# Left tiles at 0 and right tiles at 256 modulo 512 bytes: a wider edge and the constant tile first

## The chip, the cores and the metric

The kernel runs on one core of one Trainium2 chip. The metric is the device time of one execution in microseconds: 654.52 us as the median of three runs before the change (654.43 to 654.73). Engines are named as the profile names them: PE (TensorE matmuls), PEld (its weight loads), DVE (VectorE), ACT (ScalarE), POOL (GpSimd), SP (SyncE, which issues the transfers).

## What is computed

Three layers, one after the other. The first is a chunked linear recurrence over 4 x 8 sequences of 768 tokens ("attention" below), the second an MLP with an ELU, the third a gated MLP.

```python
# attention, per chunk, 8 heads of 32, state 16
CB = einsum('bhin,bhjn->bhij', Cc, Bc)
y  = einsum('bhij,bhjd->bhid', CB * L, xc) + einsum('bhin,bhnd->bhid', Cc, state) * exp(cum)
state = exp(sum(la)) * state + sum_j(Bc xc exp(cum_last - cum_j))
...
x = y as 3072 tokens x 256
h = x @ moe_w_in                          # 256 -> 2048
x = where(h > 0, h, exp(min(h, 0)) - 1) @ moe_w_out      # 2048 -> 256
g = x @ moe2_w_gate ; v = x @ moe2_w_val  # 256 -> 1536 each
out = (g / (1 + exp(-g)) * v) @ moe2_w_out               # 1536 -> 256
```

## The kernel before

The 3072 tokens are six blocks of 512. Work is laid out in a sequence of steps, one for each pair of block b and slice f of 128 features: in **phase 1** (first MLP) 6 x 16 steps, in **phase 2** (gated MLP) 6 x 12. A step issues the matmuls of its own pair and those of the pair LAG = 3 steps back; the attention work for the next block of tokens is put between the steps of phase 1 at fixed offsets, four visits to a block, and so are the decoding and splitting of weights. Engine order is the order in which the code is written (a manual schedule), with semaphores from the tile framework.

Every large product is three fp32r matmuls instead of one fp32 matmul. Each operand is split into a high and a low half (names ending in h and l), and high x high, high x low and low x high are summed. `mm3` (L493) writes these for h, g, v and o, `m_c` (L541) for c. All of them stream 512 columns (the moving operand) against 128 x 128 weights (the stationary operand, loaded anew for each matmul by a PEld instruction). Per step there are:

- phase 1, h (6 matmuls): weights `W1["i", f]` in the tiles w1h and w1l, moving xh and xl;
- phase 1, c (6): weights `W1["o", f]` in the same tiles, moving gh and gl. In block 0 it is instead two fp32 matmuls with `W1["v", f]` (L535);
- phase 2, g (6) and v (6): weights in w2h and w2l, moving x2h and x2l;
- phase 2, o (6): weights in w2h and w2l, moving gh and gl.

Where a tile lies in a partition of SBUF is set by the order in which pools are opened. Pools without a side grow from the left, in this order: `const` (ident8, con, zero_q), x2, `work` (gh, gl, m), w2e, then attention's own; when attention is done, `w2l` (w2h and w2l of f = 0 to 3) and `xs` (x2h and x2l of even blocks) take its place. Pools with `side="right"` grow downwards from the end: `edge`, a tile that nothing reads or writes, then w1p (w1h, w1l), xp (xh, xl), `stage` (raw, e, v). After phase 1 the right is closed as far as the edge, and `w2h` opens there (w2h and w2l of f = 4 to 11, x2h and x2l of odd blocks, yo). So

- h has both operands on the right, c moves from the left and has weights on the right;
- g and v have weights on the left for f < 4 and on the right from there; the moving operand is on the left for even b and on the right for odd b;
- o moves from the left always.

All these tiles are multiples of 512 bytes in size and sliced at multiples of 512, so that a side has one place modulo 512 throughout. The constants: `con` (352 words wide, of which 322 are used) holds two identities, a mask and signs; `ident8` is written once from it (L671) and read by attention's sixteen late scans (L316).

Of the kernel before, what the change touches and what calls it, by code (L numbers as in the profile page):

```python
# [8 lines left out]
F32 = mybir.dt.float32  # L9
# [38 lines left out]
WARM = 0  # L48
LEAD = 4
CON = 352  # L50
EDGE = 24
VB = 2
OX = 13
NW = 3
# [15 lines left out]
def ssm_mlp_glu_kernel(ctx, tc, a, bcs, xbc, w1, w2, consts, out):  # L70
# [4 lines left out]
    const = ctx.enter_context(tc.tile_pool(name="const", bufs=1))  # L75
    x2p = ctx.enter_context(tc.tile_pool(name="x2p", bufs=1))
    work = ctx.enter_context(tc.tile_pool(name="work", bufs=3))

    ident8 = const.tile([128, H, Q], F32, name="ident8")
    con = const.tile([128, CON], F32, name="con")  # L80
    ident_r, ident, blk_sb, sgn_sb = (con[:, x:y] for x, y in ((0, R), (R, R + Q), (R + Q, R + 2 * Q), (R + 2 * Q, R + 2 * Q + 2)))
    zero_q = const.tile([128, Q], F32, name="zero_q")
    x2_all = x2p.tile([128, 2 * NT], F32, name="x2")
# [1 line left out]

    ctx.enter_context(tc.tile_pool(name="edge", bufs=1, side="right")).tile([128, EDGE], F32, name="edge")
    right = ExitStack()
# [744 lines left out]
```

## Time and profile before

| | us |
|---|---|
| median of three runs | 654.52 |
| the profiled execution, whole | 654.61 |
| its span, first to last instruction | 652.8 |
| PE busy | 625.6 (96%) |
| PEld busy | 490.4 (75%) |
| DVE busy | 388.1 (59%) |
| POOL busy | 315.2 (48%) |
| ACT busy | 312.2 (48%) |

The granted clock of TensorE is 1.000 over the span. Matmuls are pipelined: the profile gives one of 512 columns some 390 ns, while the next starts less than 240 ns later. How fast PE goes is therefore read from start to start in the timeline, not from its busy share. In the timeline a row marked x2 stands for two instructions in a row, with the start of the first. For a mean over n gaps the rows give the first and the last start.

### The profile page before, as it was taken

The numbers are of one execution on the slowest core, as the hardware profiler recorded it, in microseconds if no ns is written. First come the engines' busy times: TensorE is split into PE (matmuls) and PEld (weight loads), VectorE is DVE, ScalarE is ACT, GpSimd is POOL, SyncE is SP. The second block draws the span as 40 slices with busy tenths as digits, with TensorE's granted clock in tenths as the row PEclk, the third lists the DMA queues.
The fourth block names the chain that finished last, engine by engine and source line by source line (L and its number), as shares of the span: only waits on it lengthen the run. The fifth ranks groups of instructions, "written<-read, shape, count | busy, mean of one in ns | idle before, by whom it ended". The sixth has DMA issues, their size and how long they took to land.

```text
span 652.8 us, 9659 instructions
## 1 busy us (share of the span) xinstructions
PE 625.6 (96%) x3620; PEld 490.4 (75%) x3620; DVE 388.1 (59%) x580; ACT 312.2 (48%) x562; POOL 315.2 (48%) x263
## 2 busy tenths in 40 slices
PE   2599999999999999999999999999999999999997
PEld 1356667777787778777788888888888888888886
DVE  5869987878887788783574663343343343343332
ACT  2146666666667666666775542322332232332322
POOL 2636657767777577764454332333233333333332
PEclk9999999999999999999999999999999999999999
DMA  6785634454344543410310000000000000000000
GB/s 181 200 286 192 171 111 143 126 151 144 127 133 132 149 133 122 133 33 19 95 50 0 2 1 1 33 0 1 32 1 1 33 1 0 34 0 2 32 1 32
DMA packets 21646, 49.54 MB, mean 76 GB/s; under 512 B 4320, under 2 KB 6496, under 8 KB 21600
## 3 DMA queue, kind: packets, MB, share of 16 engines
q1 hardware_dynamic: 21600, 48.93, 24.1%
q8 instruction: 28, 0.46, 0.3%
q14 instruction: 18, 0.15, 0.1%
HBM read 45.68 MB, written 3.24 MB: 75 GB/s over the span
## 4 chain that ended last, share of the span: by engine, by line
PE 87%; DVE 5%; issue 2%; DMA 2%; ACT 2%; SPq 1%; POOL 0%; POOLq 0%; DVEq 0%; ACTq 0%
PE h L493 18%; PE o L493 15%; PE g L493 15%; PE v L493 15%; PE c L541 14%; PE c L535 4%; DVE E L316 1%; DMA raw<-in_w 1%; PE cb L370 1%; PE y L446 1%; PE y L442 1%; DVE m L521 1%; DVE w2e L140 1%; DMA w2e<-in_xbc 1%; ACT m L515 1%
## 5 line engine op out<-in xcount | busy, mean ns | idle before, releaser
L499 POOL TENSOR_TENSOR gl<-m,gh 128x512 fp32r<-128x512 f32 x152 | 200.1, 1319 | 259.3 <-ACT gh L498 255.5
L613 DVE TENSOR_TENSOR m<-m,g 128x512 f32<-128x512 f32 x72 | 49.5, 688 | 168.5 <-ACT m L608 168.5
L608 ACT ACTIVATE m<-g 128x512 f32<-128x512 f32 x72 | 43.1, 598 | 190.5 <-PE g L493 190.5
L521 DVE SCALAR_TENSOR_TENSOR m<-m,h 128x512 f32<-128x512 f32 x96 | 65.6, 683 | 62.1 <-ACT m L520 62.1
L498 ACT ACTIVATE gh<-m 128x512 fp32r<-128x512 f32 x152 | 94.8, 624 | 1.6 <-DVE m L614 1.0
L515 ACT ACTIVATE m<-h 128x512 f32<-128x512 f32 x96 | 57.1, 595 | 69.1 <-PE h L493 64.5
L493 PE MATMUL h<-xh,w1h 128*128 128x512 f32 x192 | 80.6, 420 | 1.5 <-DVE xl L478 1.0
L493 PE MATMUL h<-xh,w1l 128*128 128x512 f32 x192 | 75.9, 395 | 0.0
L541 PE MATMUL c<-gh,w1h 128*128 128x512 f32 x160 | 63.8, 399 | 1.0 <-DVE x L547 1.0
L541 PE MATMUL c<-gh,w1l 128*128 128x512 f32 x160 | 62.4, 390 | 0.0
L520 ACT ACTIVATE m<-m 128x512 f32<-128x512 f32 x96 | 59.9, 623 | 0.5
L493 PE MATMUL h<-xl,w1h 128*128 128x512 f32 x192 | 59.9, 393 | 0.0
L493 PE MATMUL o<-gl,w2h 128*128 128x512 f32 x144 | 56.7, 394 | 0.0
L493 PE MATMUL g<-x2h,w2h 128*128 128x512 f32 x144 | 56.7, 394 | 0.0
L493 PE MATMUL o<-gh,w2h 128*128 128x512 f32 x144 | 56.6, 393 | 0.0
L493 PE MATMUL o<-gh,w2l 128*128 128x512 f32 x144 | 56.5, 393 | 0.0
L493 PE MATMUL v<-x2h,w2h 128*128 128x512 f32 x144 | 56.5, 392 | 0.0
L493 PE MATMUL g<-x2h,w2l 128*128 128x512 f32 x144 | 56.5, 392 | 0.0
L493 PE MATMUL v<-x2h,w2l 128*128 128x512 f32 x144 | 56.4, 392 | 0.0
L614 DVE TENSOR_TENSOR m<-m,v 128x512 f32<-128x512 f32 x72 | 49.5, 688 | 7.9 <-DVE m L613 0.5
L541 PE MATMUL c<-gl,w1h 128*128 128x512 f32 x160 | 50.4, 396 | 0.0
L493 PEld LDWEIGHTS h<-xh,w1h 128*128 128x128 f32 x192 | 36.4, 190 | 14.4 <-DVE m L521 3.5
(126 smaller groups left out, 1091.3 us busy)
## 6 DMA issues: line engine op xcount, KB each, us to landing
abc<-ac SPq DMA_DIRECT2D x16, 512.0 KB
bcraw<-in_bcs SPq DMA_DIRECT2D x32, 256.0 KB
raw<-in_w SPq DMA_DIRECT2D x15, 512.0 KB
w2e<-in_w SPq DMA_DIRECT2D x12, 512.0 KB
xb<-in_xbc SPq DMA_DIRECT2D x17, 256.0 KB
raw<-in_w SPq DMA_DIRECT2D x12, 256.0 KB
out_y<-yo SPq DMA_DIRECT2D x12, 256.0 KB
abc<-ac SPq DMA_DIRECT2D x8, 128.0 KB
```

Source lines behind the costliest of these rows:

```text
L140: nc.vector.tensor_scalar(halves(v)[:, :, 0], t["h16"][:, :, 1], 13, None, ALU.logical_shift_right)
L493: nc.tensor.matmul(dst, lhsT=l, rhs=r, start=first and i == 0, stop=last and i == len(ops) - 1, **kw)
L498: nc.scalar.activation(hi, src, AF.Copy)
L499: lo_eng.tensor_tensor(lo, src, hi.bitcast(F32), ALU.subtract)
L515: nc.scalar.activation(m, h, AF.Relu, scale=-1.0)
L520: nc.scalar.activation(m, m, AF.Exp, scale=-1.0)
L521: nc.vector.scalar_tensor_tensor(m, m, -1.0, h, ALU.add, ALU.max)
L535: nc.tensor.matmul(cps[b][m], lhsT=W1["v", f][:, m * 128:(m + 1) * 128], rhs=g, start=f == 0, stop=f == NF1 - 1)
L541: nc.tensor.matmul(cps[b][m], lhsT=w[:, m * 128:(m + 1) * 128], rhs=r, start=f == 0 and w is wh and r is gh, stop=f == NF1 - 1 and r is gl)
L608: nc.scalar.activation(m, pg, AF.Sigmoid)
L613: nc.vector.tensor_tensor(m, m, pg, ALU.mult)
L614: nc.vector.tensor_tensor(m, m, pv, ALU.mult)
```

## The change

Two edits. The edge grows from 24 words (96 bytes) to 56 (224 bytes), which moves every right tile down by 128 bytes. And con is allocated before ident8 rather than behind it.

```diff
-EDGE = 24
+EDGE = 56
...
+    con = const.tile([128, CON], F32, name="con")
     ident8 = const.tile([128, H, Q], F32, name="ident8")
-    con = const.tile([128, CON], F32, name="con")
```

The places, as the built programs have them (bytes from the start of a partition, and modulo 512):

| tiles | before | modulo 512 | after | modulo 512 |
|---|---|---|---|---|
| con | 20608 | 128 | 16512 | 128 |
| ident8 | 16512 | 128 | 17920 | 0 |
| zero_q, x2, work (gh, gl), w2e, w2l, xs | 22016 and up | 0 | the same | 0 |
| raw, e, v of stage; xh, xl; w1h, w1l; all of w2h | 132992 and up | 384 | 132864 and up | 256 |

Every engine has the same instructions in the same order as before.

## Rows read from the trace of the kernel before

**Rows 1.** The page's chain that ended last, shares by engine.
```profile
PE 87%; DVE 5%; issue 2%; DMA 2%; ACT 2%; SPq 1%; POOL 0%; POOLq 0%; DVEq 0%; ACTq 0%
```

**Rows 2.** Busy us (instructions) of PE, PEld, DVE, ACT, POOL; clock, DMA, by stretch.
```profile
102.00:345.80 243.80, 242.81 (x1434) 192.52 (x1431) 186.28 (x272) 164.79 (x309) 166.52 (x129) 1.00 0.36 111
345.80:648.90 303.10, 303.10 (x1315) 246.88 (x1314) 121.19 (x165) 97.13 (x167) 95.83 (x74) 1.00 0.03 9
```

**Rows 3.** PE's timeline (start, us, line, out<-moving,weights), block 1, f = 4.
```profile
412.76 0.39 PE L493 MATMUL g<-x2h,w2l 128*128 128x512 f32 x1
...
414.80 0.62 PE L493 MATMUL v<-x2l,w2h 128*128 128x512 f32 x2
```

**Rows 4.** PE's timeline, first matmul of block 2, f = 3 and f = 4.
```profile
457.87 0.39 PE L493 MATMUL g<-x2h,w2h 128*128 128x512 f32 x1
...
461.96 0.40 PE L493 MATMUL g<-x2h,w2h 128*128 128x512 f32 x1
```

**Rows 5.** PE's timeline, block 2: first matmul of f = 5, 7, 11, one more.
```profile
466.14 0.39 PE L493 MATMUL g<-x2h,w2h 128*128 128x512 f32 x1
...
474.50 0.40 PE L493 MATMUL g<-x2h,w2h 128*128 128x512 f32 x1
474.75 0.40 PE L493 MATMUL g<-x2h,w2l 128*128 128x512 f32 x1
...
491.24 0.39 PE L493 MATMUL g<-x2h,w2h 128*128 128x512 f32 x1
```

**Rows 6.** PE's timeline, block 1, f = 0 and 1.
```profile
397.19 0.40 PE L493 MATMUL v<-x2h,w2h 128*128 128x512 f32 x1
397.44 0.40 PE L493 MATMUL v<-x2h,w2l 128*128 128x512 f32 x1
...
399.97 0.40 PE L493 MATMUL g<-x2h,w2h 128*128 128x512 f32 x1
400.21 0.39 PE L493 MATMUL g<-x2h,w2l 128*128 128x512 f32 x1
400.43 0.40 PE L493 MATMUL g<-x2h,w2h 128*128 128x512 f32 x1
...
402.76 0.40 PE L493 MATMUL o<-gh,w2h 128*128 128x512 f32 x1
```

**Rows 7.** PE's timeline, first g and last o of phase 2.
```profile
345.84 0.40 PE L493 MATMUL g<-x2h,w2h 128*128 128x512 f32 x1
...
648.65 0.40 PE L493 MATMUL o<-gl,w2h 128*128 128x512 f32 x1
```

**Rows 8.** PE's timeline, phase 1, between two visits of the attention work.
```profile
127.03 0.40 PE L493 MATMUL h<-xh,w1l 128*128 128x512 f32 x1
...
137.41 0.64 PE L541 MATMUL c<-gl,w1h 128*128 128x512 f32 x2
```

**Rows 9.** PE's timeline, block 0: second h of a run, and what follows the run.
```profile
80.07 0.40 PE L493 MATMUL h<-xh,w1l 128*128 128x512 f32 x1
...
81.23 1.88 PE L535 MATMUL c<-m,v 128*128 128x512 f32 x4
```

**Rows 10.** PE's waits for DVE at L547 (us, times, longest); timeline of one.
```profile
PE c L541 <- DVE x L547: 1.0, 3, 0.6
...
149.17 0.70 DVE L304 TENSOR_TENSOR zc<-bcraw,zc 128x512 fp32r<-128x512 f32 x1
...
156.83 0.68 DVE L547 COPY x<-c 128x512 f32<-128x512 f32 x1
...
157.57 0.50 PE L541 MATMUL c<-gh,w1h 128*128 128x512 f32 x1 [0.58 <-DVE x L547]
```

**Rows 11.** Groups by line: busy us, mean ns of one, idle before.
```profile
L316 DVE TENSOR_TENSOR_SCAN E<-abc,ident 128x1024 f32<-128x1024 f32 x16 | 36.2, 2265 | 0.1
...
L579 ACT ACTIVATE w2h<-w2e 128x768 fp32r<-128x768 f32 x8 | 6.7, 837 | 0.0
...
L579 ACT ACTIVATE w2h<-w2v 128x768 fp32r<-128x768 f32 x4 | 3.3, 836 | 0.0
```

## The prediction

> **What bounds the kernel now.** I read the chain of work that ended last first: 87% of it lies on PE [rows 1]. The table by stretch comes second. In phase 1 after block 0 PE is busy for 242.81 of 243.80 us, in phase 2 for all of 303.10 us, and DVE, ACT and POOL are well below that in both [rows 2]. The granted clock is 1.00 in both, the higher of TensorE's two levels (2.4 GHz). So nobody makes PE wait; what counts is how far apart its matmuls start. I call that distance in time a gap. The busy column doesn't show it, because the recorded matmuls overlap (0.39 us each, starts 0.23 us apart). It has to be read from start times in the timeline, over many matmuls, since one start is given to 10 ns.
>
> Those gaps aren't equal, and they follow the places of the two operands. I write an arrangement as moving/stationary, by the places modulo 512 bytes given in the section on the change.
> - 384/384 (block 1, f from 4): 9 gaps from 412.76 to 414.80 are 2.04 us, 226.7 ns each [rows 3].
> - 0/0 (block 2, f = 3): 18 gaps from 457.87 to 461.96 are 4.09 us, 227.2 ns, a change of arrangement among them [rows 4].
> - 0/384 (block 2, f from 5): 108 gaps from 466.14 to 491.24 are 25.10 us, 232.4 ns [rows 5].
> - 384/0 (block 1, f = 1): 12 gaps from 399.97 to 402.76 are 2.79 us, 232.5 ns [rows 6].
>
> The instruction is the same in all four, as are its shape, the clock and what a step asks of the other engines. In odd blocks f below 4 is slow and f from 4 fast; in even blocks it is the other way round. Only the distance in place between what streams and what is loaded fits that: at distance 0 a gap is 226.7 ns, at 128 and at 384 it is 232.4, so 5.7 ns dearer.
>
> **How many are dear.** Of the 2352 fp32r matmuls (L493 and L541), h (576) has both operands on the right. c (480) streams from the left with weights on the right: dear. In phase 2, g and v have 288 at 0/384, 144 at 384/0, and 432 at distance 0; o has 288 at 0/384 and 144 at 0/0. That is 720 dear ones of 1296 in phase 2 and 1200 in all. 1200 x 5.7 ns = 6.8 us is their direct price. A change of arrangement costs a little more, since the first gaps after it are long.
>
> **What the change does, part by part.** No instruction is added, removed or moved; I cost places alone.
>
> *Right tiles from 384 to 256.* Distances 384 and 128 both become 256; distance 0 stays 0. The trace has no fp32r matmul of 512 columns at 256, so its gap is unknown. Two readings fit the rows. If the cost repeats every 256 bytes, 128 and 384 are one point, which explains why they cost the same, and 256 is the same point as 0: 226.7 ns. If it repeats every 512 and falls away evenly on both sides of 0, 128 and 384 are also alike, and 256 is anything. I take the first. Not only the means are alike at 128 and 384: single gaps of 0.25 us stand among ones of 0.23 on both sides (474.50 to 474.75 [rows 5], 397.19 to 397.44 [rows 6]), so the two arrangements seem to do the same thing in time, which an even falling-away wouldn't need. Bounds for a gap at 256: the nearest rows give 226.7 below and 0.25 us above.
>
> Phase 2: from the first g (345.84) to the last o (648.65) [rows 7] there are 1296 matmuls and 18 c of the last block of phase 1, so 1313 gaps in 302.81 us, 230.6 ns each. At 226.7 they are 297.7 us: **-5.1 us**. (Check: 720 dear ones x 5.7 = 4.1 us; the other 1.0 us is the changes of arrangement, which go as well.)
>
> Phase 1, blocks 1 to 5: 45 gaps between two visits of the attention work, 127.03 to 137.41, are 10.38 us, 230.7 ns [rows 8]. Of 960 matmuls I count some 920 such gaps; each falls by 4.0 ns: -3.7 us. Against that: after a break the gap of distance 0 isn't at once 226.7. In block 0, where h runs six at a time between other matmuls, five gaps take 1.16 us, 232 ns each [rows 9]. Phase 1 has some 24 runs; I charge each up to five gaps of 5 ns, 25 ns, so +0.6 us at most, and take +0.4: **-3.3 us**.
>
> Block 0 and all ahead of it: h is at distance 0 already and is broken up as before. I cost it at **0**; five dear gaps of 5 ns in each of 16 runs, 0.4 us, bound it on both sides.
>
> *What is late next.* PE waits for DVE at ends of blocks: three times, 1.0 us in all, for the copy of c (L547). Before the one at 157.57 DVE works without a pause from 149.17 to the end of that copy [rows 10]. What PE gains in these 8 us it waits off again: 8 us x 4.0/230.7 = 0.14 us for each of up to five block ends, so **+0.5 us** with a little for other local queues. If the whole of phase 1 went at DVE's pace instead, its 3.3 us would be lost; DVE's 186.28 busy of 243.80 [rows 2] speaks against it.
>
> *ident8 from 128 to 0, con 4096 bytes lower.* The sixteen scans that read ident8 take 2265 ns each, 36.2 us [rows 11]; DVE has room in those stretches. No row shows a scan of that size with ident8 elsewhere. I take 0, with 16 x 0.1 us of DVE time as a bound to both sides, hidden but for the local queue above. ACT and DVE also write right tiles: ACT's split of the phase 2 weights takes 837 ns where half of the tiles written lie left and half right, and 836 where all lie right [rows 11], so places don't show there.
>
> Sum: 654.61 - 5.1 - 3.3 + 0.5 = **646.7 us** against the profiled execution (span 652.8, the rest 1.8 around it). The median of the three runs is 0.09 below that execution; that is less than I can tell, and I leave 646.6.
>
> The Trainium skill, "SBUF — State Buffer", section "Who interferes with whom", speaks against any effect: it gives PE two read ports, one for the moving operand and one for LDWEIGHTS, calls them independent, and states that PE and ACT never wait on anyone. By that rule the sum would be 654.5. The trace doesn't agree: 226.7 against 232.4 ns for one instruction in two arrangements.
>
> **The rivals.**
> 1. *No gain.* The fast gap belongs to distance 0 alone, and every other distance costs 232.4. Then 1200 dear matmuls stay dear, the changes of arrangement stay, and the time is 654.5. For it: 128 and 384 are equal. Against it: the same equality is the mark of a pattern of 256 bytes. Nor do places having no part in it at all fit, since the order of fast and slow f turns round between odd and even blocks. 0.07.
> 2. *Slower.* The pattern repeats every 512 bytes and 256, farthest from 0, is its worst point. The place is the same 1200 matmuls. It is slower from a gap above 232.5 on; by 0.2% from 233.6. With the longest single gap read, about 0.24 to 0.25 us, as a constant gap: 1200 x (240 - 232.5) = 9.0 us, 663.5 us. For it: 128 and 384 are worse than 0, so farther could be worse still. Against it: they show alike rhythms, and the smooth worst point would lie at the end of a slope nothing shows. 0.07.
> 3. *Faster still.* 256 is a better point than 0. With the shortest single gap read, 0.22 us (400.21 to 400.43 [rows 6]), as a constant gap: 1200 x (226.7 - 220) = 8.0 us more, 638.6 us. No run of gaps in the rows lies below 226.7. 0.03.
>
> **How the numbers follow.** The forecast, 256 acts as 0, has 0.83. Its own range: if everything above 226.7 vanished in both phases without a charge, 5.1 + 3.7 = 8.8 us and block 0's 0.4 give 645.3; if phase 1 gives nothing, 649.5. With the bound for scans I take 645.0 to 649.8; this leaves out the rivals (0.17) and a little more, and I don't reach for them. About 0.2%, 1.3 us, is what a measurement of this kernel can tell from no change. Faster by more: 0.83 + 0.03 = 0.86; within: 0.07; slower: 0.07.
>
> **What would show it.** In the changed profile: every step of 18 matmuls in phase 2 at 4.08 us, whatever f and block (before 4.10 and 4.19 by turns); the stretch of first g to last o at 297.7 us; 45 gaps of phase 1 at 10.2 to 10.25 us; L547 making PE wait a little longer than 1.0 us in all; the start of phase 1 unchanged. Wrong in the first place: a step of odd block and f below 4, or of even block and f from 4, at 4.18 us or more. Wrong in the second: phase 2 shorter and phase 1 not, with PE's waits grown by some 3 us.

## The result

The changed kernel takes 646.82 us (median of four, 646.32 to 647.07) against 654.47 us (654.24 to 654.73) before: 7.65 us less, a ratio of 0.9882 with an interval of 0.9865 to 0.9899. The prediction was 646.6 us, with a range of 645.0 to 649.8. The profiled execution took 647.0 us with a span of 645.2.

Its page first: the span, the busy times, and the chain that ended last. It answers to [rows 1].

```profile
span 645.2 us, 9659 instructions
...
PE 617.6 (96%) x3620; PEld 490.0 (76%) x3620; DVE 387.9 (60%) x580; ACT 312.0 (48%) x562; POOL 315.1 (49%) x263
...
PE 81%; DVE 8%; DMA 3%; POOL 3%; issue 2%; ACT 2%; SPq 1%; DVEq 0%; POOLq 0%; ACTq 0%
```

The other engines are busy for as long as before; only PE's overlapped time has shrunk, by 8.0 us. PE holds 81% of the chain now instead of 87%, DVE 8% instead of 5%, POOL 3% instead of 0%: at some places the other engines come a little late now.

The table by stretch, as in [rows 2], from the same point in phase 1 to the new start of phase 2, and phase 2:

```profile
102.00:343.40 241.40, 239.76 (x1432) 192.40 (x1431) 186.11 (x272) 164.54 (x309) 166.36 (x129) 1.00 0.37 112
343.40:641.50 298.10, 298.06 (x1315) 246.48 (x1314) 121.08 (x165) 97.18 (x168) 95.78 (x74) 1.00 0.03 9
```

In phase 2 PE has next to no idle time (0.04 us) and the clock is as it was, 1.00. In phase 1 it idles for 1.6 us where it idled for 1.0.

Now the starts on PE's timeline. The first pair is first g and last o of phase 2, as in [rows 7]; the second the first g of block 1 and of block 2; the third a run of phase 1 between two attention visits, as in [rows 8]; the fourth the five gaps of block 0, as in [rows 9].

```profile
343.46 0.39 PE L493 MATMUL g<-x2h,w2h 128*128 128x512 f32 x1
...
641.07 0.39 PE L493 MATMUL o<-gl,w2h 128*128 128x512 f32 x1
...
392.42 0.39 PE L493 MATMUL g<-x2h,w2h 128*128 128x512 f32 x1
...
441.38 0.39 PE L493 MATMUL g<-x2h,w2h 128*128 128x512 f32 x1
...
126.85 0.39 PE L493 MATMUL h<-xh,w1l 128*128 128x512 f32 x1
...
137.07 0.61 PE L541 MATMUL c<-gl,w1h 128*128 128x512 f32 x2
...
80.03 0.39 PE L493 MATMUL h<-xh,w1l 128*128 128x512 f32 x1
...
81.19 0.59 PE L535 MATMUL c<-m,v 128*128 128x512 f32 x1
```

Phase 2 takes 297.61 us from first to last instead of 302.81; its 1313 gaps are 226.7 ns each. Block 1, in which slow and fast f stood side by side, takes 48.96 us for 12 x 18 matmuls, 226.7 ns again, with no dear arrangement left. In phase 1 the 45 gaps take 10.22 us (227.1 ns) instead of 10.38. Block 0 is unchanged at 1.16 us.

Where the 7.6 us of span went: phase 2 gave 5.20. From the first h of block 1 to the first g, 252.17 us (93.67 to 345.84) became 249.82 (93.64 to 343.46): 2.35. The rest, head and tail, is within 0.1.

```profile
93.67 0.79 PE L493 MATMUL h<-xh,w1h 128*128 128x512 f32 x1
```

```profile
93.64 0.79 PE L493 MATMUL h<-xh,w1h 128*128 128x512 f32 x1
```

(The first is of the kernel before, the second of the changed one: block 1's first h.)

### The profile page after: what moved, and what is told of

It is laid out like the page before. It is cut to its first block, busy times and chain, and to the rows that moved or that the text cites. A ratio compares the mean times of both kernels' runs of the same rounds, so it can differ in the third digit from the quotient of the medians.

```text
span 645.2 us, 9659 instructions
## 1 busy us (share of the span) xinstructions
PE 617.6 (96%) x3620; PEld 490.0 (76%) x3620; DVE 387.9 (60%) x580; ACT 312.0 (48%) x562; POOL 315.1 (49%) x263
## 4 chain that ended last, share of the span: by engine, by line
PE 81%; DVE 8%; DMA 3%; POOL 3%; issue 2%; ACT 2%; SPq 1%; DVEq 0%; POOLq 0%; ACTq 0%
PE h L493 16%; PE o L493 15%; PE g L493 15%; PE v L493 15%; PE c L541 12%; PE c L535 4%; DMA raw<-in_w 3%; DVE E L316 1%; POOL xb L340 1%; DVE w2e L140 1%; DVE w2e L143 1%; PE cb L370 1%; PE y L446 1%; DVE m L521 1%; DVE P L334 1%
## 5 line engine op out<-in xcount | busy, mean ns | idle before, releaser
L521 DVE SCALAR_TENSOR_TENSOR m<-m,h 128x512 f32<-128x512 f32 x96 | 65.5, 682 | 60.0 <-ACT m L520 59.9
L520 ACT ACTIVATE m<-m 128x512 f32<-128x512 f32 x96 | 59.9, 624 | 0.5
```

The source lines that it names most:

```text
L520: nc.scalar.activation(m, m, AF.Exp, scale=-1.0)
L521: nc.vector.scalar_tensor_tensor(m, m, -1.0, h, ALU.add, ALU.max)
```

## Experiments: the distance, and which edit

Theory A is the prediction's: a gap's price depends on the distance between the streamed and the loaded operand alone, and repeats every 256 bytes. Theory B: it repeats every 512, and 256 happens to be a good point. Theory C: other users of the moved tiles (ident8's scans, ACT, DVE, transfers) have part of the gain. Each time below stands beside runs of the kernel before on the same chip, 654.63 to 655.04 us, and the ratios are to these.

**Right tiles at 0.**

```diff
-EDGE = 56
+EDGE = 120
```

> The changed kernel with an edge of 120 words, which puts the right tiles at 0 modulo 512, as the left ones: distance 0 everywhere. Theory A (the cost of a gap depends on the distance between the two operands alone and repeats every 256 bytes): the same as the changed kernel, 646.3 to 647.1 us, steps of phase 2 at 4.08 us. Theory B (the cost repeats every 512 bytes and 256 only happens to be a good point too): steps at 4.08 us as well, since 384/384 and 0/0 were at 226.7 ns before; where 256 is better or worse than 0 by a little, the steps differ. Theory C (part of the gain is the move of ident8 or of the tiles that ACT, DVE and the transfers use, not of the matmul operands): a time off 646.8 by over 0.5 us with the steps of phase 2 unchanged.

Measured: 647.69 us (646.77 to 648.69), ratio to before 0.9895 (0.988 to 0.991). First g and last o:

```profile
344.80 0.39 PE L493 MATMUL g<-x2h,w2h 128*128 128x512 f32 x1
...
642.41 0.39 PE L493 MATMUL o<-gl,w2h 128*128 128x512 f32 x1
```

Phase 2 takes 297.61 us, to 10 ns what it takes at distance 256. The median is 0.9 us longer than the changed kernel's: outside theory A's range and, by the letter, theory C's sign. But it isn't lost in the stages that the places act on. In the profiled execution (648.35 us) phase 2 starts 1.3 us later, and the same 1.3 us stand already before block 1 (its first h starts at 94.91 us instead of 93.64). Two of the four runs (646.77 and 647.04) lie in A's range. Over all the profiled executions here block 1 starts between 93.14 and 94.91 us, and both extremes are kernels with distance 0 modulo 256 throughout. Why the head varies stays open; PE waits in it for transfers (5.0 and 4.3 us in the changed kernel). So the stages are compared from here on, and a time by itself only where it differs by more.

**Right tiles at 128.**

```diff
-EDGE = 56
+EDGE = 88
```

> The changed kernel with an edge of 88 words: right tiles at 128, distances 128 and 384 (the opposite signs of those of the kernel before). Theory A: 128 and 384 are one point modulo 256, so the time of the kernel before, 654.2 to 654.8 us, and steps of phase 2 at 4.10 and 4.18 us by turns as there. Theory B: near it, but no reason for equality; off by 0.5 us or more if the slope on the two sides differs. Theory C: between 646.8 and 654.5 us, since ident8 stays at 0.

Measured: 654.89 us (654.07 to 655.36), ratio 1.0001 (0.9992 to 1.0011).

```profile
345.43 0.40 PE L493 MATMUL g<-x2h,w2h 128*128 128x512 f32 x1
...
648.24 0.40 PE L493 MATMUL o<-gl,w2h 128*128 128x512 f32 x1
```

302.81 us, as before to 10 ns, with the signs of all distances turned round. Together with the first run: 0 and 256 cost the same, and so do 128 and 384. Theory B has no reason for the first. For the second it has one if its price falls away evenly on both sides of 0, since 384 is 128 on the other side; this run can't tell that from theory A, and the run at 64 bytes below can.

**Con first, edge as before.** One edit alone:

```diff
+    con = const.tile([128, CON], F32, name="con")
     ident8 = const.tile([128, H, Q], F32, name="ident8")
-    con = const.tile([128, CON], F32, name="con")
```

> The second edit alone: con before ident8, the edge left at 24 words, so the right tiles stay at 384 and only ident8 moves from 128 to 0. Theories A and B: no change, 654.2 to 654.8 us, the scans that read ident8 at 2265 ns. Theory C: faster than 654.0 us.

Measured: 654.84 us (653.88 to 655.5), ratio 1.0004 (0.9994 to 1.0013). The scans, by their group:

```profile
L316 DVE TENSOR_TENSOR_SCAN E<-abc,ident 128x1024 f32<-128x1024 f32 x16 | 36.2, 2263 | 0.1
```

2263 ns instead of 2265 [rows 11]. This edit does nothing that the runs can tell.

**Edge alone, ident8 first.**

```diff
-EDGE = 24
+EDGE = 56
```

> The first edit alone: the edge at 56 words, ident8 left ahead of con at 128. Theories A and B: all of the gain, 646.3 to 647.1 us. Theory C: slower than 647.5 us.

Measured: 647.34 us (646.9 to 647.94), ratio 0.989 (0.9875 to 0.9904): the whole gain. The median is 0.2 us above theory A's range, phase 2 again takes 297.61 us (344.36 to 641.97). Theory C falls as far as ident8 goes. As to the other users of the right tiles, this run moves them as well and doesn't decide; the next one does.

**Both sides moved by 128.** The distance stays 256, no operand lies at 0 or 256 any more.

```diff
-CON = 352
-EDGE = 56
+CON = 384
+EDGE = 24
```

> Both sides moved up by 128 against the changed kernel: con 32 words wider puts the left tiles at 128, the edge at 24 words the right ones at 384; the distance stays 256. Theory A, distance alone: 646.3 to 647.1 us, steps at 4.08 us. Rival (each operand has a place of its own that is good, 0 or 256): slower, up to 654.5 us and with steps of 4.18 us.

Measured: 647.61 us (two runs, 647.42 and 647.81), ratio 0.989 (0.9861 to 0.9919). That is 0.5 us above theory A's range. The profiled execution (647.81 us) is 0.81 longer than the changed kernel's, and 0.75 of that stand before block 1 already (its first h at 94.39 us instead of 93.64).

```profile
344.24 0.39 PE L493 MATMUL g<-x2h,w2h 128*128 128x512 f32 x1
...
641.85 0.39 PE L493 MATMUL o<-gl,w2h 128*128 128x512 f32 x1
```

297.61 us: the distance decides, not a place. With it the rest of theory C falls, since the right tiles lie at 384 as in the kernel before and the whole gain is there.

**Phase 2 alone put back.** 32 words of unused tile are opened on the right ahead of `w2h`, so that phase 2 has its right tiles at 128 and phase 1 keeps them at 256.

```diff
+ctx.enter_context(tc.tile_pool(name="edge2", bufs=1, side="right")).tile([128, 32], F32, name="edge2")
 ph2["w2h"] = ctx.enter_context(tc.tile_pool(name="w2h", bufs=1, side="right"))
```

> The changed kernel with 32 more words of unused tile on the right when phase 2's pool opens: phase 1 keeps its right tiles at 256, phase 2 has them at 128. Theory A: phase 2 takes the 302.8 us from first g to last o that it took before, phase 1 stays as after the change, 646.8 + 5.2 = 652.0 us. If the shares were otherwise (phase 1's gain larger than the 2.4 us read from the start of phase 2), the time is further from 654.5.

Measured: 652.47 us (652.01 to 653.2), ratio 0.9964 (0.9953 to 0.9975).

```profile
344.28 0.39 PE L493 MATMUL g<-x2h,w2h 128*128 128x512 f32 x1
...
646.91 0.40 PE L493 MATMUL o<-gl,w2h 128*128 128x512 f32 x1
```

302.63 us in phase 2. That is 0.2 less than before: the stretch from first g to last o begins among the last c of phase 1, whose weights stay aligned here. From the first h of block 1 to the first g it is 249.92 us (94.37 to 344.28), as after the change and not as before (249.82 and 252.17). So each phase's gain comes and goes with that phase's own places.

**Small distances.** The edge at 72, 64 and 60 words puts the right tiles 64, 32 and 16 bytes below 256. The 32 bytes were run last, with the other two known:

```diff
-EDGE = 56
+EDGE = 72
```

> The changed kernel with an edge of 72 words: right tiles at 192, distance 64 below 256. No row shows a distance that isn't a multiple of 128. If the cost rises evenly from 0 to 128 modulo 256: a mean dear gap of about 229.5 ns, phase 2 at 300 us, 650.5 us in all. If any distance but 0 modulo 256 costs the full price: 654.5 us. If the cost depends on 128-byte lines reached at the same moment and 64 lies in the same line: near 646.8 us.

```diff
-EDGE = 56
+EDGE = 64
```

> The changed kernel with an edge of 64 words: right tiles at 224, distance 32 below 256. With 16 bytes the mean gap was 233.4 ns and with 64 below 230.2, so no even rise; if a distance has its price by itself within a period of 256 bytes, between them, 231 to 233 ns, phase 2 at 302 to 303.5 us, 654 to 656 us. If 16 is dear because it isn't a multiple of 32: nearer 226.8 ns and 647 us.

```diff
-EDGE = 56
+EDGE = 60
```

> The changed kernel with an edge of 60 words: right tiles at 240, distance 16 below 256. If the cost rises evenly over 128 bytes: an eighth of the price, about 0.7 ns a gap, 647.8 us. If any distance but 0 modulo 256 costs the full price: 654.5 us. If small distances are taken up: 646.8 us.

One run each: 654.59, 656.89 and 656.53 us. First g and last o of each, in that order:

```profile
347.05 0.39 PE L493 MATMUL g<-x2h,w2h 128*128 128x512 f32 x1
...
648.59 0.40 PE L493 MATMUL o<-gl,w2h 128*128 128x512 f32 x1
```

```profile
347.19 0.39 PE L493 MATMUL g<-x2h,w2h 128*128 128x512 f32 x1
...
650.93 0.40 PE L493 MATMUL o<-gl,w2h 128*128 128x512 f32 x1
```

```profile
346.83 0.39 PE L493 MATMUL g<-x2h,w2h 128*128 128x512 f32 x1
...
650.56 0.40 PE L493 MATMUL o<-gl,w2h 128*128 128x512 f32 x1
```

| right tiles modulo 512 | distance to 0 modulo 256 | phase 2, us | mean of 1313 gaps, ns |
|---|---|---|---|
| 256, 0 | 0 | 297.61 | 226.7 |
| 240 | 16 | 303.73 | 231.3 |
| 224 | 32 | 303.74 | 231.3 |
| 192 | 64 | 301.54 | 229.7 |
| 384, 128 | 128 | 302.81 | 230.6 |

The mean is over all gaps, dear or not. An even rise, the first of the expected cases at 16 and 64 bytes, is wrong: 16 bytes off cost more than 128. Three quarters of the price of 128 bytes or more fall due at every distance tried but 0, so the good point is narrow. The three kernels with small distances were run once; their phase 2 is what is relied on.

Two readings need stretches with a single arrangement. With the right tiles at 192, the moving operand on the left and the weights on the right (block 2, f from 7 to 10), 72 gaps take 16.48 us, 228.9 ns each; the other way round (block 1, f = 1, g and v), 12 gaps take 2.80 us, 233.3:

```profile
474.96 0.39 PE L493 MATMUL g<-x2h,w2h 128*128 128x512 f32 x1
...
491.44 0.39 PE L493 MATMUL g<-x2h,w2h 128*128 128x512 f32 x1
...
400.54 0.39 PE L493 MATMUL g<-x2h,w2h 128*128 128x512 f32 x1
...
403.34 0.40 PE L493 MATMUL o<-gh,w2h 128*128 128x512 f32 x1
```

So the distance has a sign: 64 bytes cost 2.2 ns a gap when the weights lie 64 bytes lower (modulo 256) and 6.6 when the moving operand does, and the row of 64 in the table is a mixture. A price that falls away evenly on both sides, the form of theory B that was left, doesn't fit this. That the period is 256 bytes is tested at 0 against 256 and at 128 against 384, not in between.

With the right tiles at 240 the gaps where both operands lie on the right come back to the good value after the first few (block 1, f = 4: four gaps of v from 415.05 to 415.95 take 0.90 us), while 72 gaps of the left against the right (block 2, f from 7 to 10) take 16.80 us, 233.3 ns each. So it isn't the odd place 240 that is dear, but the 16 bytes between the operands:

```profile
415.05 0.39 PE L493 MATMUL v<-x2h,w2h 128*128 128x512 f32 x1
...
415.95 0.62 PE L493 MATMUL v<-x2l,w2h 128*128 128x512 f32 x2
...
475.80 0.39 PE L493 MATMUL g<-x2h,w2h 128*128 128x512 f32 x1
...
492.60 0.39 PE L493 MATMUL g<-x2h,w2h 128*128 128x512 f32 x1
```

## Experiments: what is late next in phase 1

Phase 1 gave 2.35 us where the prediction had 2.8. PE's waits of the changed kernel hold a candidate, and the timeline shows the first of the three:

```profile
PE c L541 <- DVE x L547: 1.5, 3, 0.7
...
156.06 0.39 PE L541 MATMUL c<-gh,w1l 128*128 128x512 f32 x1
157.18 0.50 PE L541 MATMUL c<-gh,w1h 128*128 128x512 f32 x1 [0.73 <-DVE x L547]
157.51 0.39 PE L541 MATMUL c<-gh,w1l 128*128 128x512 f32 x1
```

It was 1.0 us in all and 0.58 at this place [rows 10]. Theory D: take that copy out of DVE's queue and PE gets this time back. Rival E: a copy on ACT is late as well.

```diff
-        nc.vector.tensor_copy(x2[b][:, 1, :], c[1])
+        nc.scalar.activation(x2[b][:, 1, :], c[1], AF.Copy)
```

> The changed kernel itself, beside the next two on one chip: 646.8 us, PE waiting 1.5 us in all for DVE's copy of c (L547).

> The changed kernel with both halves of c copied to x2 by ACT, none by DVE (L547 becomes an activation). Theory D (the shortfall of phase 1 against the gaps is PE waiting for that copy, which stands late in DVE's queue): the waits of 1.5 us go, 645.3 to 645.8 us. Rival E (ACT's copy comes late as well, behind the activations of h, or holds these up): no change within 0.5 us, the wait now named for ACT.

> The same edit in the kernel before: theory D gives 1.0 us of waits back, some 653.5 us, so that the gain of the changed places becomes 8.1 to 8.2 us with the copy on ACT in both, against 7.7 without. Rival E: no change within 0.5 us.

Measured on one chip: 647.13 us for the changed kernel (646.73 to 647.32), 644.33 with the copy on ACT (643.74 to 644.76, ratio to before 0.9841, 0.9828 to 0.9855), 652.58 for the kernel before with the copy on ACT (652.15 to 652.77, ratio 0.9966, 0.9954 to 0.9979). The place in the changed kernel with the copy on ACT:

```profile
155.16 0.47 PE L541 MATMUL c<-gh,w1h 128*128 128x512 f32 x1
155.47 0.39 PE L541 MATMUL c<-gh,w1l 128*128 128x512 f32 x1
155.70 0.43 PE L541 MATMUL c<-gh,w1h 128*128 128x512 f32 x1
155.96 0.40 PE L541 MATMUL c<-gh,w1l 128*128 128x512 f32 x1
```

Starts 0.23 to 0.31 us apart where one stood 1.12 apart and the next 0.33: E falls, and the waits at the copy are gone as D said, but its size was wrong: 2.8 us by the medians instead of 1.0 to 1.5. One reason can be read: such a break costs more than its idle time. From 156.06 to 157.51 are 1.45 us for two gaps that would be 0.45, so 1.0 us lost for an idle time of 0.73. The idle time is counted from the recorded end of the matmul before, 0.39 us after its start, where the next would have started after 0.23; and the gap behind the break is long as well, 0.33. The stage shows less than the medians, though. From the first h of block 1 to the first g it is 249.90 us in the changed kernel on that chip (93.28 to 343.18), and 248.05 with the copy on ACT:

```profile
93.14 0.79 PE L493 MATMUL h<-xh,w1h 128*128 128x512 f32 x1
...
341.19 0.39 PE L493 MATMUL g<-x2h,w2h 128*128 128x512 f32 x1
```

That is 1.85 us. The two profiled executions differ by 1.97 us (646.73 and 644.76); what else is in the 2.8 of the medians no trace shows, and it stays open.

The second half of D has its number and not its mechanism. With the copy on ACT in both, the medians differ by 8.25 us, where D said 8.1 to 8.2. The profiled executions differ by 8.01 us (652.77 and 644.76), and 0.88 of that lies ahead of block 1 and 5.20 in phase 2. In the stage that D speaks of, the changed places are worth 249.98 - 248.05 = 1.93 us (94.02 to 344.00 in the kernel before with that edit), not more than the 2.35 with the copy on DVE. The gaps got shorter all the same, and PE waits elsewhere instead, at the end of phase 1, for DVE's ELU (L521) while phase 2's weights are decoded and split; the kernel before with that edit has neither wait:

```profile
323.88 0.50 PE L493 MATMUL h<-xh,w1h 128*128 128x512 f32 x1 [0.16 <-DVE m L521]
...
329.96 0.50 PE L493 MATMUL h<-xh,w1h 128*128 128x512 f32 x1 [0.30 <-DVE m L521]
```

Ahead of the first, DVE is held by a split of 2.09 us (L580); ahead of the second it waits itself, 0.63 us for ACT (L520). So the shortfall isn't one copy's. DVE, and once ACT behind it, set the pace over short stretches of phase 1, and a faster PE meets the next of them. This version is 2.8 us faster than the changed kernel and 10.4 us faster than the kernel before (654.68 us on the same chip).

## Why the prediction was right

Its steps in order.

*What bounds.* Right: 5.20 of 7.65 us came in a phase where PE had no idle time before or after, by starts alone.

*Distance explains the gaps.* Right, and shown: with both sides moved nothing changes, with the signs turned round at 128 nothing changes, and in phase 2 put back alone its price comes back alone. At 64 bytes the sign counts, which the rows of 128 and 384 couldn't show. One row is read too broadly: the 108 gaps given for 0/384 hold 12 of o at 0/0 (f = 2 and 3). From f = 7 on there are none, and 72 gaps from 474.50 to 491.24 are 232.5 ns, so the reading holds.

*256 acts as 0.* Right, on a guess with a reason. It was the one step without a row, and the prediction says itself that an even pattern of 512 bytes fits its rows as well. That 128 and 384 go through the same rhythm made it choose; that alone didn't exclude the other. The runs show 0 and 256 equal to 10 ns in 298 us, 128 and 384 to 10 ns in 303 us, and the unequal prices at 64 bytes speak against the even pattern.

*Phase 2, -5.1 us.* Measured -5.20. Its check, 4.1 us of dear gaps and 1.0 of changes of arrangement, is borne out too: in block 1, f = 4 to 6, every matmul was at distance 0 already, only between 384/384 and 0/0, and the 54 gaps still fall from 12.30 us (227.8 ns) to 12.24 (408.74 to 420.98 in the changed kernel). So it helps as well that the operands of neighbouring matmuls share a place modulo 256, as they do in every kernel here with 297.61 us. Before:

```profile
412.53 0.39 PE L493 MATMUL g<-x2h,w2h 128*128 128x512 f32 x1
...
424.83 0.39 PE L493 MATMUL g<-x2h,w2h 128*128 128x512 f32 x1
```

*Phase 1, -3.3 us for the gaps and +0.5 for what is late next.* Measured -2.35 together, against -2.8. The second term holds: PE's wait at the copy of c grew by 0.15 us where 0.14 was expected, and by 0.5 in all, at three block ends and not at up to five. With the copy on ACT these waits are gone, so they are that copy's. So the gaps gave about 2.9, and their term was too large by 0.4. In the long run shown they fell to 227.1 ns, as expected; but a run shortly ahead of a block's end, 151.94 to 156.06 in the changed kernel, is 18 gaps in 4.12 us, 228.9 ns. The charge for the time after a break was 25 ns a run at most and counted at less; here it is 18 x 2.2 = 40 ns. Over the whole stage the trace has 896 gaps under 0.3 us between two fp32r matmuls, 227.5 ns each (before 898, 230.9): 0.7 us above 226.7, where 0.4 was charged. That is most of the 0.4 that were missing.

```profile
151.94 0.39 PE L493 MATMUL h<-xh,w1l 128*128 128x512 f32 x1
```

*Block 0 and head, 0.* Right within what the head varies by.

*ident8 and con, 0.* Right: that edit alone is 1.0004 of before (0.9994 to 1.0013).

*The rivals.* No gain and slower both needed 256 to be dearer than 0. "Slower" was not far off as a mechanism: there are distances with a price above that of 128, but they lie at 16 and 32 bytes and not at the far end. Faster still didn't happen; no arrangement went below 226.7 ns.

*The skill's rule.* The Trainium skill, "SBUF — State Buffer", section "Who interferes with whom", has PE's two read ports independent. The runs don't agree that the two reads leave each other's timing alone: places alone move one and the same stream of matmuls between 226.7 and 231.3 ns a gap. Where on the way the streamed and the loaded operand meet, no run shows.

## What to carry to other kernels

Where fp32r matmuls with fresh weights follow each other, read the gaps from start to start and sort them by the places of the two operands; here a distance that is a multiple of 256 bytes between them saves 1.2% with not one instruction changed. An unused tile at the edge of a pool sets it, and it has to be exact: 16 bytes off lost all of the gain. No other instruction than these matmuls and no distance but those in the table was timed. When PE gets faster in a stage where another engine is locally behind, price each of PE's waits at more than its idle time.

## What the runs showed that I had not expected

- The price of a distance doesn't rise with it: in phase 2, 16 and 32 bytes cost 6.1 us, 64 bytes 3.9, 128 bytes 5.2; and 64 bytes cost 2.2 ns a gap with the weights lower, 6.6 ns with the moving operand lower.
- Phase 2 repeats to 10 ns between programs and chips (297.61 and 302.81 us, each in at least three kernels), while the head differs by up to 1.8 us.
- A wait of PE shown as 0.73 us idle cost 1.0 us, counted from start to start.
